# Attention with beacons and an ELU feed-forward layer on one core: the third batch's q and k turned by DMA transposes

## The chip, the cores and the metric

The kernel runs on one core of a Trainium2 chip. The metric is the device time of one execution in microseconds; smaller is better. The engines are named as the profile names them: PE is TensorE's matmul stream and PEld its weight loads, DVE is VectorE, ACT is ScalarE, POOL is GpSimd, and SP is SyncE, which here only issues DMAs.

## The reference

There are 8 batches of 8 heads with 576 tokens of 64 features each, and 16 extra "beacon" keys and values for each head, which every query may see. Causal attention is followed by a feed-forward layer with an ELU between its two matrices.

```python
k_all = np.concatenate([beacon_k, k], axis=2)          # 16 + 576 keys
v_all = np.concatenate([beacon_v, v], axis=2)
scores = scale * np.matmul(q, k_all.transpose(0, 1, 3, 2))
scores = np.where(causal, -1000000000.0, scores)       # beacons are never masked
a = np.exp(scores - scores.max(-1, keepdims=True))
a /= a.sum(-1, keepdims=True) + 1e-09
attn = np.matmul(a, v_all)                             # (8, 8, 576, 64)
x = attn.transpose(0, 2, 1, 3).reshape(4608, 512)
h = x @ w_in                                           # (4608, 2048)
g = np.where(h > 0.0, h, np.exp(np.minimum(h, 0.0)) - 1.0)
return g @ w_out                                       # (4608, 512), float32
```

## The kernel before, in words

The whole program is one list of words. Each word names a step and its arguments, and `run` calls the steps in the order of the list. No engine's instructions are reordered behind this: each engine executes its own instructions in the order in which the words issue them, and waits on the tiles that it reads or overwrites. So the order of the list is the schedule of PE, ACT, DVE, POOL and SP at once. A step may issue on several engines, and an engine may run far ahead of the place that its word has in the list as long as nothing that it needs is missing.

The steps that matter here, with the first argument always the batch `b` (0 to 7) or the token tile `t`:

- **Loading q and k, first way** (`lq`, `T`, `ck`, `cq`, `cb`). `lq` issues on POOL one DMA for q and one for k, which cast to bf16 and bring 576 x 64 values of each head with tokens on partitions into the staging buffers `stq[b % 2]`. `T` turns one pair of heads on PE: 24 transposing matmuls for batches after the first, into a PSUM tile with tag `S`. `ck` (ACT) or `cq` (DVE) drains that tile into `qks[p]`, and `cb` (DVE) writes the beacon columns. In the kernel before, batches 0, 1 and 2 go this way (`BD = 3`).
- **Loading q and k, second way** (`lk`, `lt`, `lp`). `lk` issues on POOL one DMA from DRAM to DRAM, which casts q or k of a batch to bf16 and puts the tokens first (tile `scr`). `lt` issues on SP two DMA transposes, one of q and one of k, for half of the heads, straight into a buffer of `stq`. `lp` writes on POOL the padding and the beacon columns of that half. In the kernel before, batches 3 to 7 go this way, all into the two tiles of `stq[1]`. The profile calls the tiles of `stq` `qst` (heads 0 to 3) and `kst` (heads 4 to 7).
- **Scores and exponentials** (`S`, `x`, `m`). `S` computes 512 columns of transposed scores for both heads of a pair (on PE) into one of two PSUM tiles with tag `S`. `x` applies the exponential on ACT into the tile `et`. `m` multiplies by the causal triangle on DVE.
- **Sums and outputs** (`D`, `L`, `n`, `W`, `M`). The sum over the keys is made by matmuls with a matrix of ones. For a batch on the second way, `D` first adds up the key blocks of `et` on DVE (four adds for each pair of heads, in place in `qks[0]` or `qks[1]`, which are free by then), and `L` needs one matmul per head for the later queries (line 419). For a batch on the first way, `L` runs over all key blocks (line 377). `n` makes the reciprocal on ACT with a logarithm and an exponential. `W` multiplies by v on PE, and `M` scales on DVE into the token tile `xT`.
- **Values and weights** (`lv`, `wi`, `wo`). `lv` issues on POOL the loads of pieces of v (five of up to 128 keys for each batch, and one small load for the beacons), `wi` those of `w_in` and `wo` those of `w_out` in four pieces. The tile of v has two buffers, so a batch's v waits for the `W` of two batches before.
- **Feed-forward** (`F`, `e`, `u`, `k`, `r`, `g`). `F` makes 128 x 512 of h on PE. `e` and `u` are exponential and relu on ACT, and `k` combines them on DVE. `r` and `g` are the same with the relu on DVE. Token tiles 0 and 1 hold 256 tokens each, the others 512.
- **Second matrix** (`G`, `o`, `s`; `Z`, `Q`, `J`, `wt`). For tiles 0 and 1 `G` is plain. From tile 2 on, `Q` is a product by Strassen's method with seven products, whose operands `Z` and `wt` prepare on DVE. `J` drains and stores.
- **Late tiles** (`H`, `X`, `P`, `K`, `E`, `U`, `V`). Parts of the first matrix for tiles 8 and 9 go by Strassen's method too. `H` prepares sums of `w_in` on DVE in the tiles `lo` and `hi`. `hi` is also where `qks[2]` and `qks[3]` lie. `X`, `P` and `K` use the space of `stq[0]`.

PSUM has two buffers of each of the tags `S`, `hps` and `ops`.

Of the kernel before, what the change touches and what calls it, by code (L numbers as in the profile page):

```python
# [17 lines left out]
def kernel(  # L18
# [11 lines left out]
    nc = tc.nc  # L30
    P = 128
# [46 lines left out]
    BD = 3  # L78
# [74 lines left out]

# [95 lines left out]
    @step  # L249
    def wi(c):  # L250
        load_wi(c)
# [149 lines left out]
    def L(b, g):  # L401
# [354 lines left out]
    @step  # L756
    def lt_(b, x_):

        t = stq[1][x_][:, 0:2 * QW].rearrange("p (y i s) -> p y i s", y=2, i=2)
        for n_ in range(2):  # L760
            nc.sync.dma_start_transpose(
                out=t[:, :, n_, NB:SK],
                in_=scr[b, n_].rearrange("s h d -> s (h d)")[:, 2 * P * x_:2 * P * (x_ + 1)])
# [3 lines left out]
    def lp(b, x_):  # L767
        t = stq[1][x_][:, 0:2 * QW].rearrange("p (y i s) -> p y i s", y=2, i=2)
# [15 lines left out]
    lq.0.0.0.4 warm.12 ident bt T.0.1.0 bk cb.0.0 wm.7 T.0.0.0 ck.0.1.0 cb.0.1 S.0.1.0  # L784
    lq.0.1.0.4 cq.0.0.0 wm.8 T.0.0.1 cb.0.2 x.0.1.0 S.0.0.0 x.0.0.0 cq.0.0.1 T.0.1.1 wm.8
    S.0.0.2 tri lq.0.0.4.8 T.0.2.0 ck.0.1.1 S.0.1.2 T.0.3.0 x.0.0.2 cq.0.3.0 cq.0.2.0 x.0.1.2
    S.0.1.1 x.0.1.1 wm.6 S.0.1.3 cb.0.3 wm.6 S.0.3.0 x.0.1.3 lq.0.1.4.8 m.0.0.2 m.0.0.0 lv.0.2
    x.0.3.0 T.0.2.1 cq.0.2.1 S.0.0.3 x.0.0.3 wm.8 S.0.2.0 T.0.3.1 x.0.2.0 S.0.2.3 x.0.2.3
    m.0.3.0 cb.1.1 wm.4 S.0.2.2 cq.0.3.1 wm.6 S.0.3.3 lq.1.0.0.4 x.0.2.2 x.0.3.3 m.0.2.0 wm.6
    S.0.0.1 x.0.0.1 m.0.1.0 L.0.A T.1.0.0 lv.0.0.1 n.0.A cq.1.0.0 m.0.0.3 T.1.1.0 W.0.A.0  # L790
    W.0.A.1 M.0.A.0 M.0.A.1 m.0.1.3 S.0.2.1 cb.1.2 ck.1.1.0 m.0.2.2 cb.1.0 S.1.5 m.0.2.3 x.0.2.1
    wi.0 x.1.5 S.1.3 x.1.3 S.0.3.1 x.0.3.1 S.0.3.2 x.0.3.2 F.0.1 e.0.1 S.1.1 r.0.1 g.0.1 S.1.4
    x.1.4 F.0.0 S.1.2 F.0.2 x.1.1 x.1.2 u.0.0 lv.0.3.4 lq.1.0.4.8 e.0.2 m.0.3.2 m.0.1.2 m.0.3.3
    L.0.B n.0.B e.0.0 wi.1 W.0.B.0 M.0.B.0 W.0.B.1 M.0.B.1 wo.0 r.0.2 T.1.2.0 F.1.1 ck.1.2.0
    g.0.2 T.1.3.0 e.1.1 u.1.1 S.1.6 x.1.6 F.0.4 F.1.7 e.0.4 k.0.0 cq.1.3.0 S.1.11 S.1.7 m.1.1.0
# [137 lines left out]
```

## Time and profile before

| | us |
|---|---|
| median of 3 runs | 337.21 |
| lowest and highest run | 336.7 and 338.57 |
| profiled execution, span from first to last instruction | 335.3 |
| PE busy in it | 324.6 |
| ACT busy | 282.5 |
| DVE busy | 280.0 |
| POOL busy | 87.9 |

The profiled execution is known by its span; the median of the runs is 1.9 us above it. Busy time of an engine is the time in which at least one of its instructions was under way. Matmuls overlap each other, so that a PE that is busy all the time need not be at its peak. The TensorE clock was granted at 0.995 of full speed on the mean. HBM was read for 37.22 MB and written for 15.34 MB, which is 157 GB/s over the span. POOL's DMAs (the profile's `software_dynamic` queue) moved 18.49 MB in 94912 packets, SP's and ACT's 15.34 MB in 33408 packets and 0.26 MB in 720.

### The profile page before, as it was taken

The page shows a single profiled execution, that of the slowest core. Times are in us where ns is not written, and L with a number is a line of the kernel's source. Part 1 is how long each engine was busy: PE and PEld are TensorE (multiplying, and loading weights), DVE is VectorE, ACT ScalarE, POOL GpSimd, SP SyncE. Part 2 cuts the span into 40 slices and gives each one's busy share as a digit, 9 for nine tenths or more (in the row PEclk, how much of TensorE's full clock was granted, in tenths as well). Part 3 has the DMA queues.
Part 4 walks back from the last instruction along what each step waited for, and adds up shares of the span by engine and source line. Part 5 has one row for each costly group of instructions (what it writes and reads, how often), then busy time and mean ns, then how long its engine had stood idle before and what let it go on. Part 6 is the DMA issues. An engine that isn't in the chain of part 4 may idle for free.

```text
span 335.3 us, 8722 instructions
## 1 busy us (share of the span) xinstructions
PE 324.6 (97%) x3561; PEld 206.8 (62%) x3561; DVE 280.0 (84%) x592; ACT 282.5 (84%) x460; POOL 87.9 (26%) x121
## 2 busy tenths in 40 slices
PE   7979899999999999999999999999999999999995
PEld 3546666454446555657555656556555888688784
DVE  3652988666899999997999889988999998998962
ACT  2998798899999999989898889897987677988930
POOL 8875749360049106500160060000000000000000
PEclk9997999999999999999999999999999999999999
DMA  9999999999939997996099495000101021010212
GB/s 114 146 174 178 165 186 186 157 147 176 149 52 170 175 139 61 171 149 105 33 140 139 104 100 139 3 33 31 39 27 34 31 65 65 31 65 31 65 63 96
DMA packets 129080, 34.65 MB, mean 103 GB/s; under 512 B 112912, under 2 KB 127504, under 8 KB 129040
## 3 DMA queue, kind: packets, MB, share of 16 engines
q0 software_dynamic: 94912, 18.49, 68.6%
q1 hardware_dynamic: 33408, 15.34, 21.2%
q8 instruction: 28, 0.46, 0.6%
q10 hardware_dynamic: 720, 0.26, 0.3%
q14 instruction: 12, 0.10, 0.1%
HBM read 37.22 MB, written 15.34 MB: 157 GB/s over the span
## 4 chain that ended last, share of the span: by engine, by line
PE 53%; DVE 20%; ACT 11%; DMA 7%; POOL 4%; issue 3%; ACTq 0%; POOLq 0%
PE ops L621 20%; PE hps L511 16%; DVE gt L536 6%; PE hps L691 6%; DVE qk L393 5%; ACT et L335 4%; ACT e L521 3%; PE sc L320 3%; PE ops L557 3%; ACT r L526 3%; PE ut L377 3%; DMA v<-in_v_dram 2%; DMA kst<-in_k_dram 2%; DMA w_out<-in_moe_w_out_dram 2%; DVE et L340 2%
## 5 line engine op out<-in xcount | busy, mean ns | idle before, releaser
L511 PE MATMUL hps<-xT,w_in 128*128 128x512 f16 (+1 forms) x544 | 120.2, 357 | 0.7 <-DMA w_in<-in_moe_w_in_dram 0.5
L335 ACT ACTIVATE et<-sc 128x1024 f16<-128x1024 f32 (+2 forms) x114 | 104.7, 978 | 5.3 <-PE sc L320 5.3
L621 PEld LDWEIGHTS <-gt 128*128 128x128 f16 x768 | 74.1, 98 | 18.7 <-issue 1.7
L521 ACT ACTIVATE e<-hps 128x512 f32<-128x512 f32 x120 | 72.5, 622 | 7.7 <-PE hps L511 5.9
L511 PEld LDWEIGHTS <-w_in 128*128 128x128 f16 x544 | 49.8, 98 | 45.3 <-issue 7.9
L536 DVE SCALAR_TENSOR_TENSOR gt<-e,r 128x512 f16<-128x512 f32 x108 | 71.9, 682 | 6.7 <-ACT r L526 4.4
L526 ACT ACTIVATE r<-hps 128x512 f16<-128x512 f32 x108 | 65.3, 623 | 7.7 <-PE hps L511 4.4
L621 PE MATMUL ops<-wt,gt 128*128 128x256 f16 x384 | 50.1, 273 | 0.0
L621 PE MATMUL ops<-w_out,gt 128*128 128x256 f16 x384 | 49.6, 273 | 0.4 <-DVE osb L635 0.3
L149 POOL DMA_DIRECT2D v<-in_v_dram x40 | 36.0, 1048 | 5.5 <-DMA w_out<-in_moe_w_out_dram 2.4
L340 DVE TENSOR_TENSOR et<-et,triu 128x512 f16<-128x512 f16 (+4 forms) x108 | 31.6, 331 | 1.5 <-ACT et L335 1.5
L578 DVE TENSOR_TENSOR gt<-gt 128x1024 f16<-128x1024 f16 x48 | 32.4, 684 | 0.3
L393 DVE TENSOR_TENSOR qk<-qk,et 128x672 f16<-128x672 f16 (+2 forms) x60 | 21.8, 368 | 0.9
L377 PEld LDWEIGHTS <-v 128*32 128x32 f16 (+1 forms) x800 | 17.0, 96 | 8.7 <-issue 0.8
L377 PE MATMUL ut<-et,v 128*32 128x464 f16 (+3 forms) x560 | 21.0, 296 | 0.0
L637 DVE TENSOR_TENSOR osb<-ops,sm 128x512 f32<-128x512 f32 x24 | 16.4, 682 | 4.3 <-issue 3.3
L471 DVE TENSOR_TENSOR xT<-ut,rl 128x672 f16<-128x672 f32 (+12 forms) x26 | 16.4, 668 | 1.7 <-ACT rl L437 1.1
L621 PE MATMUL ops<-w_out,s 128*128 128x256 f16 x128 | 17.1, 273 | 0.0
L730 DVE SCALAR_TENSOR_TENSOR gt<-e,r 128x512 f16<-128x512 f32 x24 | 16.0, 685 | 0.8 <-ACT r L720 0.7
L144 POOL DMA_DIRECT2D v<-in_beacon_v_dram x8 | 6.5, 812 | 38.4 <-PE ut L377 38.4
L557 PE MATMUL ops<-w_out,gt 128*128 128x512 f16 x64 | 16.0, 380 | 0.6 <-DMA w_out<-in_moe_w_out_dram 0.6
L621 PEld LDWEIGHTS <-s 128*128 128x128 f16 x128 | 12.4, 98 | 3.0
(108 smaller groups left out, 394.8 us busy)
## 6 DMA issues: line engine op xcount, KB each, us to landing
out_dram<-osb SPq DMA_DIRECT2D x35, 256.0 KB, 2.3
v<-in_v_dram POOLq DMA_DIRECT2D x24, 128.0 KB, 7.1
scr<-in_q_dram POOLq DMA_DIRECT2D x5, 576.0 KB, 13.8
scr<-in_k_dram POOLq DMA_DIRECT2D x5, 576.0 KB, 15.4
w_in<-in_moe_w_in_dram POOLq DMA_DIRECT2D x16, 128.0 KB, 7.5
w_out<-in_moe_w_out_dram POOLq DMA_DIRECT2D x4, 512.0 KB, 9.4
v<-in_v_dram POOLq DMA_DIRECT2D x8, 112.0 KB, 9.7
v<-in_v_dram POOLq DMA_DIRECT2D x8, 80.0 KB, 6.7
```

Of the source, the lines that this page charges most:

```text
L149: nc.gpsimd.dma_start(out=vt[b][r0:r0 + n, j, :, :], in_=v[b, :, ilo[j]:ilo[j] + n, :].rearrange("h s d -> s h d"),)
L335: nc.scalar.activation(out=ets[b, d][:, :, a - EC2 * d:e - EC2 * d], in_=sc[b, g][:, :, a - c0:e - c0], func=AFT.Exp, bias=0.0, scale=SCALE)
L340: nc.vector.tensor_tensor(out=o, in0=o, in1=i, op=ALU.mult)
L377: nc.tensor.matmul(out=t[32 * i:32 * (i + 1), a - qa:e - qa], lhsT=ones[0:kc[j], :] if half is None else v16[0:kc[j], j, h, 32 * half:32 * ...
L393: (nc.vector if eng == "v" else nc.gpsimd).tensor_tensor(out=o, in0=t[0:rows, :, a:e] if n == 0 else o, in1=t[0:rows, :, col:col + e - a], ...
L511: nc.tensor.matmul(out=h[:, n_, :], lhsT=w_in16[:, cc, P * fc:P * (fc + 1)], rhs=xt[k][:, cc, a - TT * k:e - TT * k], start=(cc == 0), sto ...
L521: nc.scalar.activation(out=eb[t, i], in_=flat(hp[t, i]), func=AFT.Exp, bias=0.0, scale=1.0)
L526: nc.scalar.activation(out=rb[t, i], in_=flat(hp[t, i]), func=AFT.Relu, bias=0.0, scale=1.0)
L536: nc.vector.scalar_tensor_tensor(out=half(t, i), in0=eb[t, i], scalar=1.0, in1=rb[t, i], op0=ALU.subtract, op1=ALU.min)
L557: nc.tensor.matmul(out=ob[t, tb_], lhsT=gt[:, fc, P * tb_:P * (tb_ + 1)], rhs=w_out16[:, fc, :], start=(fc == 0), stop=(fc == NFC - 1))
L578: (nc.vector if eng == "v" else nc.gpsimd).tensor_tensor(out=o_, in0=a_, in1=b_, op=op_)
L621: nc.tensor.matmul(out=xy[t, n_][:, qd, :], lhsT=lw[:, P * qd:P * (qd + 1)], rhs=wt_[:, c, :], start=(first and qd == 0 and c == 0), stop= ...
```

## The change

Batch 2 goes the second way instead of the first. `BD` becomes 2, so its `lq`, four `T`, two `cq`, two `ck` and four `cb` words are gone. In their place stand `lk.2.0`, `lk.2.1`, `lt.2.0`, `lt.2.1`, `lp.2.0`, `lp.2.1` and sixteen `D.2` words, and its `L` uses the sums that `D` made. The target of the DMA transposes is now `stq[b % 2]`: batches 2, 4 and 6 go to `stq[0]`, batches 3, 5 and 7 to `stq[1]`. In `load_v` the beacons' load is issued behind the load of piece 0 instead of ahead of the first piece. `wi` and `lv` words are split into one word for each load.

The list of words is the same up to `cq.1.3.0`, but for the split words. Behind that it is another order of the same steps.

```diff
-    BD = 3
+    BD = 2
...
         if b not in vt:
             vt[b] = stage.tile([P, NKC, H, D], FP16, tag="v16", name="v16")
-            nc.gpsimd.dma_start(
-                out=vt[b][0:NB, 0, :, :], in_=beacon_v[b].rearrange("h n d -> n h d"))
         for j in js:
...
+            if j == 0:
+                nc.gpsimd.dma_start(
+                    out=vt[b][0:NB, 0, :, :], in_=beacon_v[b].rearrange("h n d -> n h d"))
...
-    def load_wi(c):
+    def load_wi(c, n):
         f_ = slice(DF // 2 * c, DF // 2 * (c + 1))
-        for g in range(2):
-            for i in range(4):
-                nc.gpsimd.dma_start(
-                    out=w_in16[32 * i:32 * (i + 1), 2 * g:2 * g + 2, f_], in_=wi_v[i, :, g, :, f_])
+        g, i = n // 4, n % 4
+        nc.gpsimd.dma_start(
+            out=w_in16[32 * i:32 * (i + 1), 2 * g:2 * g + 2, f_], in_=wi_v[i, :, g, :, f_])
...
     def qk_of(b, p):
         if b < BD:
             return qks[p]
-        return stq[1][p // 2][:, 0:2 * QW].rearrange("p (y i s) -> p y i s", y=2, i=2)[:, p % 2, :, :]
+        return stq[b % 2][p // 2][:, 0:2 * QW].rearrange("p (y i s) -> p y i s", y=2, i=2)[:, p % 2, :, :]
...
-            if b >= BD:
+            if b >= 2:
                 for i in range(4):
                     nc.tensor.matmul(
...
     def lt_(b, x_):
-        t = stq[1][x_][:, 0:2 * QW].rearrange("p (y i s) -> p y i s", y=2, i=2)
+        t = stq[b % 2][x_][:, 0:2 * QW].rearrange("p (y i s) -> p y i s", y=2, i=2)
...
     def lp(b, x_):
-        t = stq[1][x_][:, 0:2 * QW].rearrange("p (y i s) -> p y i s", y=2, i=2)
+        t = stq[b % 2][x_][:, 0:2 * QW].rearrange("p (y i s) -> p y i s", y=2, i=2)
```

The list of words from the end of the common part to the fourth batch's scores, before:

```
k.0.0 cq.1.3.0 S.1.11 S.1.7 m.1.1.0 cb.1.3 r.0.4 g.0.4 e.1.7 r.1.7 lq.2.0.0.8 G.0.0.0 x.1.7 F.0.5
x.1.11 e.0.5 S.1.12 g.1.7 cb.2.1 m.1.2.0 x.1.12 S.1.0 F.0.7 r.0.5 G.0.1.0 S.1.8 x.1.0 g.0.5 F.1.5
e.0.7 x.1.8 m.1.3.1 S.1.10 cb.2.0 m.1.1.1 S.1.9 e.1.5 x.1.10 r.0.7 g.0.7 cb.2.2 lv.1.0.1 wo.1 r.1.5
g.1.5 x.1.9 F.1.0 u.1.0 e.1.0 m.1.0.0 T.2.0.0 cq.2.0.0 F.0.3 T.2.1.0 cq.2.1.0 T.2.2.0 e.0.3 u.0.3
m.1.2.1 k.0.3 wt.1.0 k.1.1 ck.2.2.0 F.1.4 F.0.6 e.0.6 S.2.0 S.2.5 x.2.5 x.2.0 r.0.6 m.1.3.0 G.0.0.1
m.1.0.1 g.0.6 G.0.1.1 k.1.0 lv.1.2.3.4 lp.3.0 lp.3.1 T.2.3.0 e.1.4 ck.2.3.0 L.1.1 n.1.1 F.1.2 ...
M.1.1.0 W.1.1 M.1.1.1 S.2.3 F.1.3 x.2.3 L.1.0 W.1.0 n.1.0 wo.2 M.1.0.0 M.1.0.1 u.1.3 e.1.3 wo.3 ...
S.2.1 x.2.1 F.2.13 wt.1.1 e.2.13 S.2.4 lk.3.0 lk.3.1 lt.3.0 ... lv.2.2.3.4 ... lv.2.0.1 e.1.6 G.1.0.2
S.3.0 x.3.0 S.2.11 x.2.11 F.2.9 F.2.15 ... lk.5.1 ... lk.4.0 ... S.3.2 S.3.3 x.3.3
```

and after:

```
k.0.0 cq.1.3.0 m.1.0.1 lk.2.0 r.0.4 S.1.12 lv.1.0 e.1.7 S.1.11 g.0.4 r.1.7 g.1.7 x.1.12 H.1.1 x.1.11
F.1.3 e.1.3 m.1.1.0 F.1.5 m.1.1.1 H.1.0 e.1.5 r.1.5 S.1.7 u.1.3 S.1.0 lk.2.1 x.1.0 G.0.0.0 cb.1.3
lv.1.1 lv.2.2 g.1.5 x.1.7 lv.1.4 k.1.3 F.0.5 m.1.2.0 F.0.3 e.0.5 u.0.3 m.1.3.1 r.0.5 e.0.3 S.1.8
S.1.10 lp.2.0 k.1.1 G.0.1.0 x.1.8 m.1.0.0 g.0.5 F.0.7 lp.2.1 S.1.9 H.2.0 x.1.10 F.1.0 x.1.9 m.1.3.0
lv.1.3 u.1.0 m.1.2.1 e.0.7 L.1.0 e.1.0 n.1.0 lv.1.2 L.1.1 n.1.1 wo.1 r.0.7 g.0.7 M.1.0.0 k.1.0 k.0.3
F.1.2 lv.2.4 wo.3 M.1.1.0 u.1.2 F.0.6 e.0.6 W.1.0 W.1.1 e.1.2 wo.2 lk.3.0 lk.3.1 lt.2.0 M.1.0.1 r.0.6
g.0.6 S.2.3 M.1.1.1 x.2.3 F.1.4 G.0.1.1 e.1.4 lt.2.1 S.2.1 S.2.2 x.2.1 F.2.1 r.1.4 g.1.4 G.0.0.1 x.2.2
u.2.1 e.2.1 F.2.3 e.2.3 lv.3.4 S.2.4 S.2.5 x.2.4 F.2.7 wt.1.0 r.2.3 G.0.1.2 x.2.5 S.2.6 S.2.0 G.0.1.3
wt.2.0 e.2.7 m.2.0.1 H.1.2 g.2.3 lv.2.0 F.2.11 x.2.6 lt.3.0 u.2.7 k.1.2 lv.2.1 lv.2.3 m.2.1.1 k.2.7
m.2.1.0 o.0.1 x.2.0 lk.4.0 e.2.11 u.2.11 m.2.0.0 F.2.13 e.2.13 u.2.13 S.2.7 D.2.0.0 D.2.1.0 ...
lp.3.1 ... lk.4.1 ... lk.6.1 S.2.10 lp.4.0 e.2.0 lv.3.2 ... lk.5.0 S.2.9 ... lp.3.0 ... L.2.0 ... S.3.4
```

More of the change, by code (lines that the diff above doesn't have):

```diff
@@ L249, in wi @@
     @step
-    def wi(c):
-        load_wi(c)
+    def wi(c, n):
+        load_wi(c, n)
     @step
@@ new lines @@
+    cq.0.0.0 wm.8 T.0.0.1 cb.0.2 x.0.1.0 S.0.0.0 x.0.0.0 cq.0.0.1 T.0.1.1 wm.8 S.0.0.2 tri
+    lq.0.0.4.8 T.0.2.0 ck.0.1.1 S.0.1.2 T.0.3.0 x.0.0.2 cq.0.3.0 cq.0.2.0 x.0.1.2 S.0.1.1 x.0.1.1
+    wm.6 S.0.1.3 cb.0.3 wm.6 S.0.3.0 x.0.1.3 lq.0.1.4.8 m.0.0.2 m.0.0.0 lv.0.2 x.0.3.0 T.0.2.1
+    cq.0.2.1 S.0.0.3 x.0.0.3 wm.8 S.0.2.0 T.0.3.1 x.0.2.0 S.0.2.3 x.0.2.3 m.0.3.0 cb.1.1 wm.4
+    S.0.2.2 cq.0.3.1 wm.6 S.0.3.3 lq.1.0.0.4 x.0.2.2 x.0.3.3 m.0.2.0 wm.6 S.0.0.1 x.0.0.1 m.0.1.0
+    L.0.A T.1.0.0 lv.0.0 lv.0.1 n.0.A cq.1.0.0 m.0.0.3 T.1.1.0 W.0.A.0 W.0.A.1 M.0.A.0 M.0.A.1
@@ new lines @@
+    Z.4.1.0 S.5.10 S.6.2 u.5.1 Q.4.0.7 lv.5.3 x.6.2 Z.4.1.1 k.5.5 F.5.0 D.5.0.3 k.5.12 x.5.10
+    Q.4.7.14 m.5.2.1 m.5.3.1 Q.4.14.21 e.5.0 u.5.0 S.6.4 S.6.0 u.5.15 lt.7.0 J.4.0.v k.5.1 lp.7.1
+    D.5.1.0 e.5.15 F.5.3 x.6.4 x.6.0 m.5.3.0 Q.4.21.28 m.6.0.1 D.5.1.1 Z.4.2.0 k.5.15 D.5.1.2
+    Z.4.2.1 D.5.1.3 F.5.4 u.5.3 e.5.3 S.6.1 x.6.1 W.5.0 lt.7.1 u.5.4 L.5.0 k.5.3 e.5.4 k.5.0 k.5.4
+    n.5.0 Q.4.28.35 F.5.13 e.5.13 F.5.10 Z.4.4.0 J.4.1 u.5.13 e.5.10 Q.4.35.42 M.5.0.0 k.5.13
+    D.5.2.0 F.5.11 u.5.10 u.5.11 F.5.8 D.5.3.0 e.5.11 u.5.8 m.6.1.0 e.5.8 m.6.0.0 M.5.0.1 D.5.2.1
@@ new lines @@
+    U.8.0.5.v V.8.0.4 P.8.1.3 P.8.1.4 V.8.0.6 Z.7.2.0 K.8.1.3 Z.7.1.1 K.8.1.4 E.8.1.1 W.7.0 W.7.1
+    U.8.1.1 P.8.1.5 Q.7.14.21 M.7.0.1 K.8.1.5 J.7.0 P.8.1.6 P.8.2.0 U.8.1.4 E.8.1.6 Q.7.21.28
+    V.8.1.1 U.8.1.6 E.8.1.4 K.8.2.0 Q.7.28.35 V.8.0.5 P.8.2.1 Z.7.2.1 V.8.1.4 K.8.2.1 P.8.2.2
+    E.8.1.5 Q.7.35.42 P.8.2.3 K.8.2.2 U.8.2.1 K.8.2.3 U.8.1.5 P.8.2.4 J.7.1 Q.7.42.49 V.8.1.6
+    P.8.2.5 M.7.1.1 K.8.2.4 E.8.2.1 K.8.2.5 J.7.2 V.8.2.1 Q.7.49.56 V.8.1.5 U.8.2.4 P.8.2.6 F.8.14
+    Q.7.56.63 E.8.2.6 U.8.2.6 u.8.14 e.8.14 F.8.15 F.8.13 V.8.2.6 E.8.2.4 Z.7.4.1 k.8.14 e.8.15
@@ L904 @@
+    k.9.12 u.9.14 Q.9.0.7 Z.9.1.0 V.9.2.4 F.9.13 e.9.14 k.9.15 e.9.13 u.9.13 Q.8.98.105 Q.8.105.112
+    k.9.14 J.8.6 Z.9.3.1 k.9.13 Q.9.7.14 Q.9.14.21 Z.9.1.1 Z.9.2.1 Z.9.2.0 Q.9.21.28 J.9.0 Q.9.28.35
+    Q.9.35.42 J.9.1 Q.9.42.49 J.9.2 Q.9.49.56 Q.9.56.63 Q.9.63.70 Q.9.70.77 Z.9.4.1 J.9.3 Z.9.4.0
+    Q.9.77.84 Q.9.84.91 J.9.4 Q.9.91.98 Q.9.98.105 J.9.5 Q.9.105.112 Jh.9.0 Jh.9.1
     """)
```

217 lines of the change are left out of this document (97 added, 120 removed).

## The prediction

> **What bounds the kernel now.** First the page's busy line, then busy time by stretch, then the PE, POOL and SP timelines and the DMA issues asked for one stretch at a time.
>
> ```profile
> PE 324.6 (97%) x3561; PEld 206.8 (62%) x3561; DVE 280.0 (84%) x592; ACT 282.5 (84%) x460; POOL 87.9 (26%) x121
> ...
> DMA  9999999999939997996099495000101021010212
> ...
> 40.00:60.00 20.00, 19.70 (x298) 13.07 (x301) 16.61 (x35) 18.12 (x25) 13.24 (x16) 1.00 1.68 183
> 60.00:76.00 16.00, 15.96 (x172) 7.78 (x165) 9.98 (x22) 14.76 (x23) 8.70 (x7) 1.00 2.20 157
> 76.00:94.00 18.00, 18.00 (x228) 8.40 (x226) 13.31 (x28) 17.02 (x29) 0.25 (x1) 1.00 1.81 142
> 94.00:130.00 36.00, 36.00 (x358) 20.24 (x357) 34.44 (x76) 35.58 (x59) 14.46 (x18) 1.00 1.35 125
> ```
>
> In a row by stretch stand the stretch, its length, then PE, PEld, DVE, ACT and POOL busy, granted clock, DMA share and GB/s. PE never rests after 40 us, and as the starts in its timeline follow each other at the pace of the columns (four 512-column matmuls of L511 every 0.86 us), it is truly occupied: added up word by word at their usual spacing, PE's work from 38.1 us on is 289.6 us, and it took about 293. So PE sets the end, and any wait of PE after 40 us is paid in full. But the DMA engines are saturated too until about 94 us; DVE has room from 60 to 94 us (10.7 us idle) and almost none from 94 to 130 (1.6 us).
>
> ```profile
> 47.88 1.53 POOL L165 DMA_DIRECT2D w_out<-in_moe_w_out_dram  x2 [2.60 <-DMA kst<-in_k_dram]
> 49.40 2.24 POOL L754 DMA_DIRECT2D scr<-in_q_dram  x1
> 51.11 2.76 POOL L754 DMA_DIRECT2D scr<-in_k_dram  x1
> ...
> 62.91 5.58 SPq L761 DMA_TRANSPOSE qst<-scr  x2
> ...
> 77.50 0.39 PE L320 MATMUL sc<-qst 64*128 64x512 bf16 x2
> ...
> qst<-scr SPq DMA_TRANSPOSE x2, 9.4
> kst<-scr SPq DMA_TRANSPOSE x2, 10.4
> ```
>
> POOL's loads wait for the landing of the load eight places earlier (47.88 us: w_out behind the third batch's k, eight loads before). Asked one by one, POOL's loads land in the order of issue: w_out piece 0 at 40.2 us (32.43 + 7.8), q and k of the third batch at 43.4 and 47.6, the fourth batch's scr loads at 62.8 and 66.5 (49.40 + 13.4, 51.11 + 15.4), so one scr load occupies the queue 3.7 us, a v piece 0.85 us (52.5, 53.3; the short last piece 0.57), a w_out piece 2.5 us. The last two rows are the transposes issued from 40 to 94 us: 9.4 and 10.4 us from issue to landing. In the late, drained stage one issued at 187.15 us takes 3.5 us. The fourth batch's first pair is issued at 62.91 and 66.58, lands at 72.1 and 76.2, and PE's first fourth-batch scores start at 77.5: 1.3 us of margin.
>
> **The change, part by part. PE.** It loses four T words of the third batch:
>
> ```profile
> 49.11 0.45 PE L266 MATMUL tp<-identb,qst 96*64 96x96 bf16 x12
> 49.38 0.42 PE L266 MATMUL tp<-identb,kst 96*64 96x96 bf16 x12
> 49.64 0.45 PE L266 MATMUL tp<-identb,qst 96*64 96x96 bf16 x12
> ...
> 55.13 0.90 PE L377 MATMUL lt<-et,ones 128*32 128x464 f16 x24
> ...
> 112.17 0.37 PE L419 MATMUL lt<-qk,ones 128*32 128x464 f16 x4
> ```
>
> One T takes 0.53 us beside another (49.11 to 49.64) and 0.64 before other work: 4 x 0.6 = 2.4 us. Two L words shrink from 0.93 us (55.13 to the next word's start at 56.06) to 0.45 (112.17 to 112.62): 1.0. Together 3.4. Adding up the new order's PE words in the same way, each at the median spacing that before shows for its kind ahead of the next one's kind, gives 287.1 instead of 289.6, a gain of 2.5. I take 3.0; the bounds are 2.5 and 3.4.
>
> **DVE** gets sixteen adds of the third batch, 4 x (633 + 501 + 370 + 234) ns = 7.0 us by the L393 rows, and loses two drains (2 x 1357 ns, L279) and four beacon copies (4 x 158 ns, L275), 3.3 in all: +3.6 us. In the new order they stand between PE words that come at 66 and 82 us, where 10.7 us were idle: nothing. If late scores push them past 94 us, the cover is 1.6 us and up to 2.0 come on the path. Three H words moved to 40 to 48 us (six adds of 282 ns) fit in DVE's 3.4 us of idle time there. **ACT** loses two drains of 1.1 us, work beside PE: nothing. Alternating buffers free the later transposes from waiting for the preceding batch's scores, but PE is busy 36.00 of 36 us there: nothing. Moving the beacon v load behind v piece 0 only exchanges places among the first loads: nothing, +/- 0.3.
>
> **POOL and DMA.** Two loads straight to SBUF (issue 0.79 us, at 33.20) become two to DRAM (issue 2.2 us): +2.9 us of POOL, idle 6.8 of 20 us there. In the queue they cost 3.7 each against 3.2 and 4.2: even. Four transposes are new work for saturated engines. Their price is read from the queue's delay in before: from 66.5 to 93.8 us POOL's landed loads (beacons, seven v pieces, three scr) are worth 17.0 us and took 27.3; in that time lay four transposes and two 256 KB outputs, the latter worth 1.2 each by w_out's 512 KB in 2.5. (10.3 - 2.4) / 4 = 2.0 us per transpose. From below: the scr load landing at 66.5 came 3.7 us after its predecessor although a transpose was in flight, so 0; from above 2.5, with all of the loss laid on them. I take 2.0.
>
> **Where PE waits.** New landings, in the new order of POOL: w_out 0 at 40.2, third batch's q 44.0, v 1.0 and beacon 44.7, k 48.4, five v pieces 52.4. The SP queue has nothing ahead of lt.2.0, so its pair is issued at 44.0 and 48.4 and lands, with 9.6 us as the pair's second took in before, at 58.0. PE: F.1.7 starts at 38.1 as before; ahead of S.2.3 come nine F (0.95 us), seven S (0.28), two G and two L (0.87 each), two W (1.43): 55.0. It waits 3.0 us. W.1.0 at 52.1 needs the v pieces of 52.4, later by what the transposes take: the same wait, met a little sooner. From S.2.3 on, thirteen S, twelve F (0.92), ten G (0.89) and L.2.0 (0.35) lead to S.3.4 at 78.9. Its pair of transposes landed at 76.2 in before; now come before it four transposes (+8.0) and v 2.2 and 2.4 (+1.4), and one output transfer is gone from there (-1.2): 84.4. PE is 5.5 us late at that point, S.2.3's 3.0 included. On POOL, lp.3.0 (beacon columns for S.3.4) stands behind lp.4.0, which waits for the third batch's scores, and behind lv.3.2 and lk.5.0, which wait for v landings: about 82, so the transposes end last. After 94 us the engines have gaps and nothing else is late. Sum: 5.5 - 3.0 = +2.5 us.
>
> The profiled execution is known by its span, 335.3 us; the runs' median, 337.21, is 1.9 above it, and I add the difference to the median: **339.7 us**.
>
> **The rivals.** (1) The transposes behave in the saturated stage as in the drained one: 3.5 us to landing and nothing lost to POOL's loads. Then lt.2.0 lands at 51.9, before PE asks at 55.0, lt.3.0 before 78.9, and the PE gain stays: 337.2 - 3.0 = 334.2, faster. It decides as soon as a transpose costs the queue under 0.6 us ((78.9 - 76.2 - 1.4 + 1.2) / 4). For it speaks the scr load at 66.5, against it 9.4 and 10.4 us and the 10.3 us lost. [...] (2) Only the wait at S.2.3 is real and S.3.4's data come in time: 3.0 - 3.0, no change, 337.2. For it: the v loads that delayed the fourth batch's transposes in before are now partly behind them. (3) Worse than forecast: 2.5 us per transpose, the output still there, lands at 87.6, PE is 8.7 us late and D.2's adds lose their cover (2.0): 337.2 + 8.7 + 2.0 - 3.0 = 344.9.
>
> **How the numbers follow.** What a measurement of this kernel can tell from no change is about 0.5%, 1.7 us. Forecast 0.42, rival 1 0.34, rival 2 0.16, rival 3 0.08. Faster 0.34, same 0.16, slower 0.50. Signs are mixed, so: the forecast's own range runs from 338.5 (1.7 us a transpose, gain of 3.0) to 342.2 (2.5 us, gain of 2.5); the full range from rival 1, 333.8 with a gain of 3.4, to 343.5, which leaves out most of rival 3.
>
> **What would show it.** PE timeline: no `tp` for the third batch, 96 fewer transposing matmuls, L.2 with L419; PE waits released by DMA at the first `sc` of the third batch (near 55 us) and of the fourth (near 80 us), some 5 us together; DMA issues of the stretch 40 to 90 us with transposes at 9 us or more. If the first eight transposes land 4 us after issue and PE shows no DMA wait after 40 us, the forecast is wrong and rival 1 holds. If PE waits instead on ACT or DVE after 94 us, the step on DVE's cover is wrong.

## The result, and the profile after

The changed kernel is slower: a median of 350.19 us (345.97 to 351.96) against 337.22 us; the ratio is 1.03, with a 95% interval from 1.0239 to 1.036, about 10 us. (The runs of one kernel fall into a faster and a slower group: a ratio compares the faster ones alone, a median takes in all runs.) The forecast was 339.7 us with a range to 343.5. The direction was the likelier one, and the size was off by a factor of four: +2.5 us were forecast. Its profiled execution took 345.97 us, with a span of 344.3 us against 335.3.

First the page of the kernel after: the engines' busy line, and the granted TensorE clock and the DMA share in 40 slices.

```profile
PE 325.1 (94%) x3433; PEld 206.9 (60%) x3433; DVE 281.6 (82%) x602; ACT 279.8 (81%) x458; POOL 92.3 (27%) x125
...
PEclk9999996969999999999999999999999999999999
DMA  9999999999999999969089509400010020021112
```

PE has 128 matmuls fewer and yet is as long busy, because two of the slices ran at a clock of 0.6; and the DMA engines, which before had a slice at 0.3 from 92 to 101 us, now have none under 0.9 until 146 us. The same stretches as before (stretch, length, then PE, PEld, DVE, ACT and POOL busy, granted clock, DMA share, GB/s):

```profile
40.00:60.00 20.00, 15.71 (x218) 10.03 (x220) 12.04 (x33) 12.96 (x21) 10.35 (x13) 0.86 1.87 157
60.00:76.00 16.00, 13.01 (x92) 5.30 (x83) 8.95 (x20) 9.90 (x14) 5.91 (x8) 0.82 1.95 151
76.00:94.00 18.00, 15.75 (x114) 7.02 (x112) 13.78 (x31) 14.45 (x24) 9.20 (x12) 0.93 1.88 168
94.00:130.00 36.00, 36.00 (x374) 19.11 (x373) 31.40 (x67) 34.16 (x55) 15.48 (x18) 1.00 1.99 151
```

PE rests 9.5 of the 54 us from 40 to 94, where it rested 0.3, and the clock is under 1 in three rows that stood at 1.00. The PE timeline of the kernel after tells where (start, us, what; in brackets the idle time before it and what ended it):

```profile
38.77 2.16 PE L511 MATMUL hps<-xT,w_in 128*128 128x256 f16 x16 [1.00 <-DVE gt L548]
...
56.32 4.59 PE L377 MATMUL ut<-et,v 128*32 128x336 f16 x72 [4.28 <-DMA v<-in_v_dram]
...
68.66 1.02 PE L557 MATMUL ops<-w_out,gt 128*128 128x512 f16 x4 [0.61 <-DMA w_out<-in_moe_w_out_dram]
...
72.28 0.40 PE L320 MATMUL sc<-kst 64*128 64x256 bf16 x2 [2.38 <-DMA kst<-scr]
...
88.02 0.38 PE L419 MATMUL lt<-qk,ones 128*32 128x464 f16 x4
...
93.49 0.61 PE L320 MATMUL sc<-qst 64*128 64x192 bf16 x10 [2.25 <-POOL qst L770]
```

38.77 is F.1.3, waiting for DVE ahead of this stretch; 56.32 is W.1.0, waiting for the second batch's v piece 2; 72.28 is S.2.6, for the third batch's k of heads 4 to 7 (`lt.2.1`); 93.49 is S.3.4, for POOL's `lp.3.0`. L.2.0 is the short form (88.02). The transposes of the kernel after, issued from 40 to 94 us (median us from issue to landing), and their places on SP's queue:

```profile
qst<-scr SPq DMA_TRANSPOSE x5, 8.6
kst<-scr SPq DMA_TRANSPOSE x4, 13.3
```

```profile
42.67 6.02 SPq L761 DMA_TRANSPOSE qst<-scr  x2
48.80 14.11 SPq L761 DMA_TRANSPOSE kst<-scr  x2
73.63 5.54 SPq L761 DMA_TRANSPOSE qst<-scr  x2
```

One by one, the four new ones were issued at 42.67, 47.12, 48.80 and 55.28 us and landed at 51.52, 59.76, 66.69 and 72.14: 9 to 18 us each. Last, POOL's timeline in the kernel after:

```profile
73.92 2.19 POOL L754 DMA_DIRECT2D scr<-in_q_dram  x1 [7.27 <-issue]
...
77.63 4.42 POOL L754 DMA_DIRECT2D scr<-in_k_dram  x2 [1.18 <-issue]
...
90.81 2.19 POOL L754 DMA_DIRECT2D scr<-in_q_dram  x1 [7.62 <-issue]
92.49 0.70 POOL L769 MEMSET qst<- 128x96 bf16 x1
92.61 0.83 POOL L770 COPY qst<-bkT 128x32 bf16<-128x32 bf16 x1
```

POOL stands still for 7.3 and 7.6 us with nothing to wait for that the trace names ("issue"). Each time it goes on 0.3 us behind the landing of an earlier scr load (73.57, 77.32 and 90.48 us). The last two rows are `lp.3.0`, which stands in the list behind `lk.5.0`, the load that POOL could not issue.

**Ledger.** From the start of F.1.7 to PE's last instruction took 293.2 us before (38.1 to 331.3) and 304.2 us after (36.2 to 340.4; its opening happened to run 1.9 us ahead): +11.0. PE's idle time in that stretch is 11.35 us, where before had 1.62: 1.00 + 4.28 + 0.61 + 2.38 + 2.25 = 10.5 are the waits above, the rest gaps of 0.35 us and less. The trace's clock records grant 0.5 from 54.46 for 6.83 us and from 71.52 for 6.83 us; PE worked in 4.97 and 6.07 us of them, and at half clock half of that is lost (eight 512-column matmuls of L511 took 3.62 us at 74.72, at full clock 1.89 us at 80.57), 2.5 + 3.0 = 5.5. So 9.7 + 5.5 = 15.2 us came on, and 11.0 are seen: PE's own work, without its idle time and without what the clock lost, fell from 291.6 to 287.3 us, by 4.3 and not by the 3.0 of the forecast.

### The profile page after: what moved, and what is told of

It reads as the page before. It is cut to its first block, busy times and chain, and to the rows that moved or that the text cites. A ratio compares the mean times of both kernels' runs of the same rounds, so it can differ in the third digit from the quotient of the medians.

```text
span 344.3 us, 8501 instructions
## 1 busy us (share of the span) xinstructions
PE 325.1 (94%) x3433; PEld 206.9 (60%) x3433; DVE 281.6 (82%) x602; ACT 279.8 (81%) x458; POOL 92.3 (27%) x125
## 4 chain that ended last, share of the span: by engine, by line
PE 65%; DMA 14%; POOL 8%; issue 6%; ACT 3%; DVE 3%; DVEq 0%; POOLq 0%
PE ops L621 27%; PE hps L511 22%; DMA v<-in_v_dram 6%; DMA w_out<-in_moe_w_out_dram 6%; PE hps L691 5%; PE sc L320 5%; PE ut L377 4%; POOL scr L754 3%; DMA kst<-in_k_dram 2%; ACT et L335 1%; POOL v L147 1%; POOL qst L136 1%; PE ops L557 1%; POOL kst L136 1%; ACT r L526 1%
## 5 line engine op out<-in xcount | busy, mean ns | idle before, releaser
L511 PE MATMUL hps<-xT,w_in 128*128 128x512 f16 (+1 forms) x544 | 119.4, 358 | 1.3 <-DVE gt L548 1.2
L335 ACT ACTIVATE et<-sc 128x1024 f16<-128x1024 f32 (+2 forms) x114 | 104.5, 985 | 16.9 <-PE sc L320 16.8
L511 PEld LDWEIGHTS <-w_in 128*128 128x128 f16 x544 | 51.1, 98 | 44.9 <-issue 6.8
L536 DVE SCALAR_TENSOR_TENSOR gt<-e,r 128x512 f16<-128x512 f32 x108 | 72.5, 683 | 5.4 <-ACT r L526 2.5
L147 POOL DMA_DIRECT2D v<-in_v_dram x40 | 38.3, 1027 | 63.0 <-PE lt L377 53.3
L377 PEld LDWEIGHTS <-v 128*32 128x32 f16 (+1 forms) x800 | 18.5, 100 | 14.4 <-DMA v<-in_v_dram 4.7
L377 PE MATMUL ut<-et,v 128*32 128x464 f16 (+3 forms) x560 | 23.0, 316 | 4.3 <-DMA v<-in_v_dram 4.3
L393 DVE TENSOR_TENSOR qk<-qk,et 128x672 f16<-128x672 f16 (+2 forms) x72 | 25.5, 366 | 0.5
L754 POOL DMA_DIRECT2D scr<-in_q_dram x6 | 13.3, 2212 | 17.0 <-issue 15.2
L754 POOL DMA_DIRECT2D scr<-in_k_dram x6 | 14.4, 2468 | 11.8 <-DMA scr<-in_q_dram 7.3
L320 PE MATMUL sc<-qst 64*128 64x336 bf16 (+13 forms) x192 | 14.8, 256 | 2.7 <-POOL qst L770 2.2
L393 DVE TENSOR_TENSOR qk<-et 128x928 f16<-128x928 f16 x24 | 14.9, 633 | 2.6 <-PE lt L419 2.4
```

Of the source, the lines that this page charges most:

```text
L147: nc.gpsimd.dma_start(out=vt[b][r0:r0 + n, j, :, :], in_=v[b, :, ilo[j]:ilo[j] + n, :].rearrange("h s d -> s h d"),)
L320: nc.tensor.matmul(out=s[:, h, a - c0:e - c0], lhsT=t[D * h:D * (h + 1), 1, P * j:P * (j + 1)], rhs=t[D * h:D * (h + 1), 0, NB + qa + a - ...
L335: nc.scalar.activation(out=ets[b, d][:, :, a - EC2 * d:e - EC2 * d], in_=sc[b, g][:, :, a - c0:e - c0], func=AFT.Exp, bias=0.0, scale=SCALE)
L377: nc.tensor.matmul(out=t[32 * i:32 * (i + 1), a - qa:e - qa], lhsT=ones[0:kc[j], :] if half is None else v16[0:kc[j], j, h, 32 * half:32 * ...
L393: (nc.vector if eng == "v" else nc.gpsimd).tensor_tensor(out=o, in0=t[0:rows, :, a:e] if n == 0 else o, in1=t[0:rows, :, col:col + e - a], ...
L511: nc.tensor.matmul(out=h[:, n_, :], lhsT=w_in16[:, cc, P * fc:P * (fc + 1)], rhs=xt[k][:, cc, a - TT * k:e - TT * k], start=(cc == 0), sto ...
```

## The experiments

**Theory A**: the transposes take 2 to 3 us each from POOL's saturated load queue; PE's waits for late loads, the half clock behind each, and POOL's stop ahead of `lp.3.0` are the loss, and the PE gain is real. **Rival B**, in its several forms: the half clock costs nothing of its own because PE has to wait for loads anyway; or the new order of words, not the transposes, is what costs; or the loads are late as a whole, so that what is won at one wait is lost at the next. Times are ratios to the kernel before on the same chip, with the 95% interval.

| run | ratio | interval |
|---|---|---|
| e1_beacon: before, beacons' load moved | 1.0005 | 0.9978 to 1.0032 |
| e7_altbuf: before, alternating buffers | 1.0007 | 0.9986 to 1.0028 |
| e6_sums: before, third batch summed on DVE | 1.0100 | 1.0073 to 1.0127 |
| e8_lt2_old_order: before, transposes alone | 1.0448 | 1.0405 to 1.0491 |
| e11_lt3_twice: before, four more transposes | 1.0076 | 1.0044 to 1.0107 |
| e2_no_lt2: after, without the four transposes | 1.0057 | 1.0029 to 1.0085 |
| e3_pe_busy: after, fillers in the waits | 1.0433 | 1.0397 to 1.0469 |
| e4_lp3_first: after, lp.3.0 early | 1.0252 | 1.0213 to 1.0290 |
| e5_both: e4 with fillers | 1.0257 | 1.0210 to 1.0303 |
| e9_fill: e4 with own work in the waits | 1.0291 | 1.0248 to 1.0335 |
| e10_no_lt2_lp3: e2 and e4 together | 0.9884 | 0.9846 to 0.9923 |
| e13_v3_first: e10, one scr load later | 0.9918 | 0.9882 to 0.9955 |
| e12_t_on_pe: after's order, third batch on PE | 1.0138 | 1.0087 to 1.0189 |

### The parts that were costed at nothing: e1_beacon, e7_altbuf

Each is one hunk of the diff, put alone into the kernel before.

> The kernel before, with one part of the change alone: the beacons' v load issued behind v piece 0. Theory A (this move is what made the changed kernel's opening 2.1 us shorter: the last w_in piece landed at 24.4 instead of 25.6 us, PE no longer paused, and the half clock granted from 25.3 to 28.8 us in before did not come): no grant of 0.5 near 25 us, PE starts its second T.1 pair about 2 us earlier, 335.2 us, a gain of 0.4 to 0.7%. Rival B (the two traces differ there by chance): the same as before, 337.2 us, with the half clock still there.

> The kernel before with one part of the change: the DMA transposes of batches 3 to 7 go to stq[b % 2] instead of always stq[1]. Theory A (PE is busy 36.00 of 36 us behind 94 us, nobody waits for a buffer): within 0.5% of 337.2 us. Rival B (a transpose that may start earlier takes away the waits for scores of the fourth batch on, seen as 0.87 us on a kst tile at 154 us in the run with the sums): 335 us or less.

336.84 and 337.74 us. Neither moves the time: both intervals hold 1 and reach no further than 0.32% from it. The trace of e1 does show what its theory A foretold, no grant of 0.5 near 25 us and the T.1 pair 1.4 us earlier (33.10 against 34.52), but so does the trace of e7 (33.01), which lacks the move. So the 1.9 us by which the profiled opening of the kernel after was ahead are not shown to come from the beacons' load.

### Without the third batch's transposes: e2_no_lt2

```diff
-    ... lk.3.1 lt.2.0 M.1.0.1 ... e.1.4 lt.2.1 S.2.1 ...
+    ... lk.3.1 M.1.0.1 ... e.1.4 S.2.1 ...      (stq[0] set to zero on DVE)
```

> The changed kernel with the third batch's four DMA transposes left out (its scores are then made from buffers set to zero by two VectorE memsets in the opening). All loads of POOL and the order of words stay. Theory A (the four transposes hold up POOL's loads by 10 us, and all PE waits after 40 us and the two half-clock grants follow from that): v 1.2 lands near 51.5 us instead of 56.3, the fourth batch's k near 67 instead of 77, no PE wait over 0.7 us after 40 us, no grant of 0.5 after 40 us; span 330 to 333 us, time 332 to 335. Rival B (the new order asks for its loads too early whatever the transposes do): waits at W.1.0 and S.3.4 of 2 us or more stay, 339 us or more.

338.72 us: most of the loss is gone, though theory A's 332 to 335 us are missed. From 41 us on PE waits for nothing over 0.6 us, until S.3.4. The fourth batch's k, which landed at 77.32 us in the kernel after, lands at 68.83 although the loads of this opening ran 1.9 us later (the third batch's k at 48.92 against 47.06): 10.4 us for four transposes, 2.6 each. The one wait left, in the PE timeline of e2_no_lt2:

```profile
84.94 1.03 PE L320 MATMUL sc<-qst 64*128 64x192 bf16 x10 [4.49 <-POOL qst L770]
```

POOL's `lp.3.0` again, behind `lk.5.0`, which goes out when the scr load of `lk.4.0` has landed (81.99 us). That is a second cause, beside the transposes.

### Fillers against the half clock: e3_pe_busy, and `lp.3.0` early: e4_lp3_first

```diff
+            if (b, g) == (1, 0):
+                fill(t[:, 0, :], 20)          # matmuls into the tile that W.1.0 is about to write
+    FILLS = {(2, 6): 20, (3, 4): 24}          # the same ahead of S.2.6 and S.3.4
```
```diff
-    ... k.2.13 lp.3.1 m.2.2.0 ... D.2.0.3 lp.3.0 x.2.10 ...
+    ... k.2.13 lp.3.1 lp.3.0 m.2.2.0 ... D.2.0.3 x.2.10 ...
```

> The changed kernel with PE kept busy where it waits: 20 extra matmuls of 512 columns ahead of W.1.0 and of S.2.6 and 24 ahead of S.3.4, into PSUM that the real ones then overwrite. Theory A (the half clock costs 5.5 us of PE work in the changed kernel's trace, but S.3.4 is held by POOL's lp.3.0 at 93.4 us, which follows from DMA landings alone, so the 5.5 us turn into a longer wait at S.3.4): no grant of 0.5 between 50 and 80 us, S.3.4 still at 93 to 94 us, span 343 to 345 us as with the change. Rival B (the half clock is a loss of its own): S.3.4 at 88 us and the span near 339 us.

> The changed kernel with the word lp.3.0 moved ahead, directly behind lp.3.1, so that POOL writes the fourth batch's beacon columns at about 75.6 us instead of 92.5. Theory A (POOL could not go past lk.5.0, because its queue was full until lk.4.0 had landed at 90.5 us, and PE's wait of 2.3 us at S.3.4 ends with lp.3.0): S.3.4 starts when PE comes to it, about 91.2 us, waiting for nothing, as its transposes landed at 85.9; span 342 us, 2.3 us less than with the change. Rival B (the transposes' data end that wait, as the prediction had it): S.3.4 stays at 93.5 us and the span at 344 us.

e3 had no stretch at 0.5 while PE worked (mean clock 0.999) and took 351.25 us, more than either theory had. Its PE and POOL timelines:

```profile
92.53 5.34 PE L312 MATMUL sc<-w_in 128*128 128x512 f16 x24
```

```profile
94.31 2.19 POOL L765 DMA_DIRECT2D scr<-in_q_dram  x1 [8.27 <-issue]
...
96.12 0.86 POOL L781 COPY qst<-bkT 128x32 bf16<-128x32 bf16 x1
```

PE comes to the fillers in front of S.3.4 at 92.5 us and ends them at 97.9, but POOL's copy ends only at 97.0: without fillers POOL's stop would have held S.3.4 until then. So e3 can't price the half clock. e4 takes the stop away: 345.18 us, 6 us under e3; against the kernel after (1.0252 and 1.03) the intervals overlap, so that what the stop cost after is seen in the traces and not in the time. S.3.4 starts at 91.3 us without a wait. What is left from 41 to 94 us, in its PE timeline:

```profile
57.18 4.11 PE L377 MATMUL ut<-et,v 128*32 128x336 f16 x72 [3.37 <-DMA v<-in_v_dram]
...
61.85 0.40 PE L320 MATMUL sc<-qst 64*128 64x48 bf16 x6 [0.56 <-DMA qst<-scr]
...
69.53 1.02 PE L557 MATMUL ops<-w_out,gt 128*128 128x512 f16 x4 [0.67 <-DMA w_out<-in_moe_w_out_dram]
...
73.58 0.28 PE L320 MATMUL sc<-kst 64*128 64x256 bf16 x2 [2.80 <-DMA kst<-scr]
```

7.4 us of waits, and two stretches of 3.41 us at 0.5 (from 57.50 and 74.57), 1.7 us lost in each. F.1.7 to PE's end took 300.8 us, 7.6 more than before.

### Half clock without POOL's stop: e5_both, and the waits filled with own work: e9_fill

e5 is e4 with 20 fillers at W.1.0 and 10 at S.2.6. e9 is e4 with these moves:

```diff
-    F.0.6 e.0.6 W.1.0 W.1.1 e.1.2 ... x.2.3 F.1.4 G.0.1.1 ... S.2.6 S.2.0 ... F.2.11 ... F.2.13 ...
+    F.0.6 e.0.6 e.1.2 F.1.4 W.1.0 W.1.1 ... x.2.3 G.0.1.1 ... S.2.0 ... F.2.11 ... F.2.13 S.2.6 ...
```

> The kernel after with the beacon copies lp.3.0 right behind lp.3.1 and with filler matmuls in two waits of PE (20 at W.1.0, 10 at S.2.6; their results are overwritten). Without the fillers this kernel had a span of 342.6 us and two stretches of 3.4 us at a granted clock of 0.5. Theory A (half clock behind a wait of PE is a loss of its own, half of such a stretch each): no such stretch, the fourth batch's S.3.4 starts 2 to 3 us earlier than without the fillers (88.4 to 89.4 instead of 91.4 us), span 339.5 to 341, median 342 to 343.5. Rival B (PE has to wait for the loads anyway, so that a faster clock only makes the next wait longer): S.3.4 within 1 us of 91.4, span 342 to 343.5, median 345.

> The kernel after with lp.3.0 right behind lp.3.1, and its own work put into PE's waits: F.1.4 moved ahead of W.1.0, S.2.6 moved behind F.2.13. Theory A (what is left of the loss is waits for landings at W.1.0 and S.2.6 and the half clock behind them; work moved into them is won back): S.3.4 starts at 88.5 to 90 us instead of 91.4, median 341 to 343.5. Rival B (landings at the end of the chain of loads, lt.3.0 and the fourth batch's, set S.3.4 whatever PE does before): S.3.4 within 0.7 us of 91.4 and the median near 345.

In e5 both stretches at 0.5 are gone and S.3.4 starts at 89.0 us instead of 91.3, as theory A had it. But the time is 346.44 us, as rival B had it. The 2.3 us are given back at 121 us, in the PE timeline of e5_both:

```profile
121.60 0.38 PE L386 MATMUL lt<-et,v 128*32 128x112 f16 x8 [2.90 <-DMA v<-in_beacon_v_dram]
...
123.80 1.73 PE L386 MATMUL ut<-et,v 128*32 128x208 f16 x28 [0.77 <-DMA v<-in_v_dram]
```

These are L.3.0 and W.3.0, waiting for the fourth batch's v, with 6.83 us at 0.5 from 120.83 on. e9 is no better (347.58 us): its moves put new waits in the place of the old, 2.07 us for ACT at 55.8 and 2.29 for w_out at 70.3, each with 3.41 us at 0.5; S.3.4 starts at 90.6, and 2.44 and 0.71 us of waiting follow at 122.6 and 124.1. So the half clock, once gone, let PE come 2.3 us earlier to S.3.4, and the lateness of the loads, which reaches to 125 us, took that back. Both theories were half right.

### Both causes away: e10_no_lt2_lp3, and one scr load moved: e13_v3_first

e10 joins the edits of e2 and e4. e13 adds one move:

```diff
-    D.2.3.1 lk.5.1 F.2.12 ... lv.3.0 ... lp.4.1 W.2.0 lv.3.3 u.2.4 ...
+    D.2.3.1 F.2.12 ... lv.3.0 ... lp.4.1 W.2.0 lv.3.3 lk.5.1 u.2.4 ...
```

> The kernel after without the four transposes of the third batch (its tiles in stq[0] are set to zero on VectorE instead, so its scores are not the reference's) and with lp.3.0 right behind lp.3.1. Theory A (two causes: transposes that hold the loads up, and the fourth batch's beacon copies behind a blocked POOL; with both gone the PE gain of the prediction shows): no PE wait over 1 us between 41 and 94 us, span 331 to 333, median 331.5 to 334, faster than before by 1 to 1.7%. Rival B (the loads are late further on as well and PE, now earlier, meets them at the fourth batch's v near 110 us): a wait of 2 us or more there, median 335.5 to 338.

> The kernel e10_no_lt2_lp3 (no transposes of the third batch, zeros in its tiles, lp.3.0 early) with the scr load lk.5.1 moved behind the fourth batch's v pieces lv.3.0 and lv.3.3. Theory A (PE's wait of 2.9 and 1.6 us at 112.8 us is the turn of one scr load of 3.7 us in POOL's queue): the fourth batch's v lands 3.5 to 4 us earlier, that wait is under 1 us, no half clock behind it, span 330 to 331.5, median 331.5 to 333. Rival B (the queue is late as a whole, and another load is met next): a wait of 2 us or more elsewhere between 94 and 140 us, median 334 or more.

e10 is the first version that beats before (ratio 0.9884; it leaves out the third batch's q and k, so it is a measure of what the transposes cost, and no kernel to use). Its seven runs lie from 331.94 to 339.46 us, with a median of 335.77. No PE wait over 0.5 us between 41 and 94 us; S.2.3 at 56.0 and S.3.4 at 80.2, where the prediction's sum had PE at 55.0 and 78.9 without waits. The run that was traced is the longest of the seven, and it shows what rival B said; whether the shorter ones had this wait too is not shown. The PE timeline of e10 and then of e13:

```profile
112.80 0.28 PE L377 MATMUL lt<-et,v 128*32 128x112 f16 x8 [2.92 <-DMA v<-in_beacon_v_dram]
112.90 0.72 PE L377 MATMUL ut<-et,v 128*32 128x464 f16 x12
115.22 1.73 PE L377 MATMUL ut<-et,v 128*32 128x208 f16 x28 [1.60 <-DMA v<-in_v_dram]
```

```profile
110.72 0.27 PE L377 MATMUL lt<-et,v 128*32 128x112 f16 x8
110.99 1.51 PE L377 MATMUL ut<-et,v 128*32 128x464 f16 x40
...
129.47 0.61 PE L320 MATMUL sc<-qst 64*128 64x512 bf16 x8 [0.97 <-DVE osb L637]
```

In e10 the beacons' v lands at 112.67 behind `lk.5.1`'s scr load (111.75); with that load moved behind it, it lands at 107.74, and PE waits for no load from 42 us on. F.1.7 to PE's end takes 290.4 us (38.8 to 329.3), 2.8 us under before's 293.2. That is not the PE gain alone: PE still waits for DVE, 1.00 us at 41.45 and 0.97 at 129.47, and has 3.1 us of idle time in all, 1.5 more than before. So the gain in PE's own work is 4.3 us here too. In time, though, e13 is not shown better than e10 (0.9918 and 0.9884, intervals overlapping; 334.64 us where A had 331.5 to 333). Its executions have spans from 331.0 to 339.8 us; in the profiled one F.1.7 started 0.7 us later than in before. What makes the openings differ stays open.

### The pieces in the old order: e8_lt2_old_order, e6_sums; one more measure of a transpose: e11_lt3_twice

```diff
 e8:  BD = 2; transposes of the third batch into stq[0]; L sums on PE for b < 3
-    ... r.1.7 lq.2.0.0.8 G.0.0.0 ...                  (T, cq, ck, cb of batch 2 gone)
+    ... r.1.7 lk.2.0 lk.2.1 lp.2.0 lp.2.1 lt.2.0 lt.2.1 G.0.0.0 ...
 e6:  if b >= 2: (short L);  sixteen D.2 words from k.2.11 on, W.2.1 ahead of L.2.1, wt.2, wt.4, H.1.1 later
 e11:
-    ... lt.3.0 ...
+    ... lt.3.0 tc.3.0 tc.3.1 ...      (tc: the same transposes once more, into stq[0]; nobody reads them)
```

> The kernel before in its own order of words, only the third batch's q and k brought by scr loads and DMA transposes (into the free staging buffer); the sums stay on PE. Theory A (the third batch's transposed tiles land at 58 us or later whatever the order of PE's words, and each transpose holds POOL's loads up by 2.4 to 2.7 us): PE waits 6 us or more at S.2.0, half clock behind it, fourth batch's scores late as well; 343 to 350 us. Rival B (the new order of words is what costs, the transposes themselves little): 334 to 338 us.

> The kernel before, with the third batch's q and k still turned on PE, but its exp tiles summed on VectorE (sixteen adds, and L.2 needs one matmul a head). Theory A (the sums are the good half of the change, each shortened L word worth 0.48 us on a PE that sets the end, DVE's adds covered): 1.0 to 1.9 us faster, median 335.1 to 336. Rival B (DVE's adds of 7.0 us lose their cover in this order, or PE's gain is met by a later wait): 336.9 or up to 1 us slower.

> The kernel before with four more DMA transposes that nobody reads: behind the fourth batch's first pair the same data go a second time, all four halves, into stq[0], which is free there. Theory A (in the stretch in which POOL's queue is full each transpose takes 2.4 to 2.7 us from POOL's loads): the third scr load that lands at 93.8 us in before lands at 103 to 105; 2 to 8 us slower. [...]

e8: 352.68 us, slower than the whole change, so the transposes cost without the new order too. The wait at S.2.0 (59.18) is 3.35 us, shorter than expected because PE was itself late: one DVE instruction took 3.99 us (35.16 to 39.15; 0.42 to 1.5 in the other runs) while POOL issued the two scr loads, and PE waited 2.95 us behind it. With it went 13.65 us at 0.5 in three stretches. That DVE instruction makes e8's sum larger than the transposes' own cost. In the DVE and then the PE timeline of e8:

```profile
35.16 3.99 DVE L543 TENSOR_SCALAR r<-e 128x512 f16<-128x512 f32 x1
```
```profile
39.93 3.08 PE L511 MATMUL hps<-xT,w_in 128*128 128x256 f16 x16 [2.95 <-DVE gt L548]
```

e6 refuted its theory: 341.11 us, 1% slower, where theory A had 1.0 us of gain or more and even rival B at most 1 us of loss. Busy time by stretch in e6 (columns as above):

```profile
76.00:94.00 18.00, 15.34 (x178) 7.36 (x177) 16.67 (x40) 14.90 (x24) 0.00 (x0) 1.00 1.51 126
```

DVE went from 13.31 us to 16.67 of 18, and PE waited 1.17 us for `gt` and 1.24 for `xT` of DVE. Sixteen adds of 7 us are free only where DVE's other work isn't due. In the changed kernel's order no PE wait of over 0.4 us was for DVE from 41 us on; e6 says nothing of other places for the adds.

e11: 339.27 us, 0.76% slower. The last scr load of the stretch lands at 100.60 us instead of 93.83, in an opening that ran 1.6 us earlier (v pieces at 72.07 and 73.64): 8.3 us for four transposes, 2.1 each, a little under theory A's 103 to 105. With that, the price is 2.1 to 2.6 us (e11 and e2).

### The new order with the third batch on PE: e12_t_on_pe

```diff
-    ... lk.2.0 ... lk.2.1 ... lt.2.0 ... lt.2.1 ...  D.2.*  H.1.1 H.1.0 H.2.0 H.1.2
+    ... lq.2.0.0.8 ... T.2.0.0 cq.2.0.0 ... T.2.1.0 ck.2.1.0 ... T.2.2.0 ck.2.2.0 ... T.2.3.0 cq.2.3.0 ...
```

The moves of `lp.3.0` and `lk.5.1` are kept, and the H words stand behind the third batch's scores.

> The order of the kernel after, with the third batch's q and k turned on PE again and its sums on PE (no D.2 words, H words later), lp.3.0 right behind lp.3.1 and lk.5.1 behind lv.3.3; nothing left out. Theory A (with no transposes in the full queue the new order is as good as the old, and its sums and turns on PE cost 3.4 us against e13_v3_first): no PE wait over 1.5 us behind 41 us, 335 to 337 us, same as before or a little faster. Rival B (the new order leans on the fast third batch; the drains of the turned tiles on VectorE and ScalarE hold PE up instead): several waits of PE on DVE or ACT between 48 and 75 us, 339 us or more.

341.72 us, rival B: no wait for a load, but PE waits of 1.71, 0.85, 0.59 and 0.74 us for ACT and DVE at 54.0, 57.6, 68.8 and 76.1 us. That the turned tiles' drains stand in the way of `e` and `gt` there is the likely reading; it was not tried by itself. One arrangement was run; no complete kernel that beats before was found.

## Why the prediction was wrong

**Right.** PE sets the end and pays every wait. From F.1.7 to PE's last instruction, in us (lost to the clock: half of the time that PE worked at 0.5; PE's own work: what is left):

| | length | PE idle | lost to the clock | PE's own work |
|---|---|---|---|---|
| before | 293.2 | 1.6 | 0 | 291.6 |
| after | 304.2 | 11.4 | 5.5 | 287.3 |
| e4_lp3_first | 300.8 | 9.8 | 3.4 | 287.6 |
| e2_no_lt2 | 296.1 | 6.3 | 2.5 | 287.3 |
| e10_no_lt2_lp3 | 296.1 | 7.3 | 1.4 | 287.4 |
| e13_v3_first | 290.4 | 3.1 | 0 | 287.3 |

The five kernels in the new order have the same PE words, and PE's own work comes out the same to 0.3 us, although idle time and slow clock together differ by 14 us among them. That is what shows that the waits and the half clock make up the loss. Buffers and beacons at nothing: e7 and e1. A transpose at 2.0 us, bounds 0 to 2.5: 2.1 to 2.6. The rival by which transposes cost nothing is refuted. The landing of `lt.3.0`, forecast for 84.4, was 85.94; but the opening was 1.9 us ahead, so that it came 3.4 us later than the sum had it. The third rival's 344.9 us came near the time by luck, for the 2.0 us that it gave to DVE's adds did not arise. The loads lost 2.1 to 2.6 us to each transpose, where w_out's 512 KB in 2.5 us would put a plain transfer of as many bytes, half of a scr load's 576 KB, at 1.4 (an estimate).

**The PE gain.** The 3.0 us, with bounds of 2.5 and 3.4, were too small: PE's own work fell by 4.0 to 4.3. The sum by words was near for the new order (287.1, measured 287.3) and 2.0 us short for before (289.6, measured 291.6). Which words of before cost more than their usual spacing was not followed up.

**Where PE waits, the step at W.1.0 and S.2.3.** "The same wait, met a little sooner" was mis-sized. The v pieces were put at 52.4 us, "later by what the transposes take", and that was never added: piece 2 landed at 56.28, and the wait is 4.3 us where 3.0 were summed. Nothing was left for S.2.3.

**The step that was missing: `lt.2.1`.** The sum followed only the first pair. The second was issued at 48.80 and 55.28 and landed 17.9 and 16.9 us later, and S.2.6 waited 2.4 us. Pricing the transposes at 9.6 us to landing, as a single pair had taken in before, did not hold for four in a row between the loads: they took 8.9, 12.6, 17.9 and 16.9.

**The term that was missing: the half clock.** The waits of 4.28 and 2.38 us in after came with 6.83 us at 0.5 each, those of 3.37 and 2.80 us in e4 with 3.41 each; the 2.25 us ahead of S.3.4 in after came with none. The two stretches of after lost 5.5 us in the profiled execution, as much again as the whole forecast lateness. The row of before from 20 to 30 us (granted clock 0.83) already showed such a stretch behind the opening's gaps; it was not read.

**POOL, the step on `lp.3.0`.** "About 82" was 93.4, since `lk.5.0` ahead of it could not be issued: 2.25 us of PE's time in after, 4.49 in e2. So POOL ended last at S.3.4, and not the transposes, which had landed at 85.94. In before the same stop can be seen, harmlessly, at 74.05 us (2.71 us).

**DVE, the step on the cover.** Right for this order (from 41 us on no PE wait of over 0.4 us was for DVE), though e6 shows that the nothing hung on where the adds stand.

In all, the waits were put at 5.5 us and PE's idle time grew by 9.7, the half clock was put at nothing and took 5.5, and the PE gain was put at 3.0 and was 4.3. That is 4.2 + 5.5 - 1.3 = 8.4 us short, where 8.5 are seen (11.0 - 2.5).

## What to carry to other kernels

Where the load queue is saturated, price a new transfer by what it delays, and follow the whole queue to where it drains: here a lateness of some 10 us went from v to `kst` to POOL's copies to the next v, and what was won at one wait in e5 and e9 was lost at a later one. Price PE's longer waits with the slow clock that the traces show behind them: here 3.41 or 6.83 us at 0.5 for waits of 2.38 to 4.28 us, though none for the 2.25 us ahead of S.3.4. Count all of PE's idle time, on both sides, before calling what is left a gain: in e13 1.5 us of small waits hid a third of it. Work taken from PE was no gain where the engine or queue that got it had no room in that very stretch: e6's adds left DVE busy 16.67 of 18 us, and the time grew by 1%.

## What the runs showed of the hardware

- **The clock.** In after, PE waited 4.28 us up to 56.32 and 2.38 us up to 72.28, and the granted clock was 0.5 from 54.46 and from 71.52 us, for 6.83 us each. In before it was 0.5 from 25.35 us for 3.41 us, with PE idle in four gaps of 0.73, 0.52, 0.56 and 0.52 us between 21.93 and 25.70. The waits of 2.25 us at 93.49 and of 1.00 us at 38.77 in after came with no grant below 1. At 0.5 PE's work took about twice as long: eight 512-column matmuls of L511 3.62 us at 74.72 in after, and 1.89 us at 80.57, at full clock. What decides whether such a stretch comes, and how long it is, was not tried by itself and stays open.
- **POOL's loads stop.** With several scr loads outstanding POOL did not issue the next for up to 8.3 us (e3), and in after it went on 0.3 us behind a landing each time (at 73.92, 77.63 and 90.81 us). What stops it was not tried by itself and stays open.
- **DVE beside POOL's issue.** One DVE instruction of 0.42 us took 3.99 us in e8, just while POOL issued two scr loads. It was seen once, and the cause stays open.
